# The head of a fused attention and gated-MLP kernel: x tile 0 in halves on two queues, a one-block first weight piece, a new matmul order and a fourth gate/up slot

## Chip, cores, metric

One core of one Trainium2 chip. The metric is the device time of one execution in microseconds, median of several. The kernels ran on several chips; each ran beside the kernel before on its own chip, and is compared with those runs only.

## Reference

```python
xn = layernorm(x)                                  # x: 2048 x 512, bf16
s  = attention(xn @ wq, k_cache, v_cache) @ wo     # 32 heads, 2048 keys, head size 128
h  = relu(xn @ W_gate) * (xn @ W_up)               # 512 -> 1792
g  = silu(h @ W_down)                              # 1792 -> 512
return x + s * g
```

## The kernel before

The kernel runs the MLP first, for four blocks of 512 rows, then the attention. Only the start of the MLP (the "head") is touched. The first block has no normalized x yet, so its four x tiles of 128 rows are only centred (the row scale is applied later), transposed on TensorE into the PSUM banks `ps_acc`, copied by ScalarE (ACT) to `xcT`, and multiplied with the first three column blocks of both weights, tile by tile (`head_tile`). Column block 3 and later ones are full width, 512 columns. The gate and up results stand in three slots of two PSUM banks each.

```python
FCS = [0, min(3, FC), min(8, FC), FC]      # weight pieces: 3, 5 and 6 column blocks
HFC = 3                                    # column blocks that run tile by tile
warm_w = sem_ln1.sig(dve.memset(warm[:], 0.0))
load_x0(sp, 0)                             # x tile 0, 128 KB
load_x0(act, 1)
load_w(sp, Wg_sb, wg_src, sem_wg, 0)       # 384 KB
load_w(act, Wu_sb, wu_src, sem_wu, 0)      # 384 KB
load_x0(sp, 2)
load_x0(act, 3)
load_w(sp, Wg_sb, wg_src, sem_wg, 1)
load_w(sp, Wu_sb, wu_src, sem_wu, 1)
... # x of block 1, the last weight pieces, the other x blocks, W_down: all on sp

def head_ln():
    ctok = {0: head_transpose(0, head_center(0))}
    warm_mm(2)
    for n in range(4):
        if n + 1 < 4:
            ntok = head_center(n + 1)      # DVE: statistics, aggregation, centring
        _wait(pe, ctok[n])                 # xcT copy of tile n
        head_tile(n, 0)
        if n + 1 < 4:
            ctok[n + 1] = head_transpose(n + 1, ntok)
        for fc in range(1, HFC):
            head_tile(n, fc)               # 4 gate and 4 up matmuls, 128 x 128

... # emit_gate_up, for column blocks from HFC on:
s = ring_acquire()                         # waits until slot s has been read out
... # 4 gate matmuls and 4 up matmuls of 128 x 512
... # main:
_wait(pe, warm_w)
warm_mm(10)                                # filler matmuls, 128 x 512, to raise the clock
head_ln()
```

The softmax here doesn't subtract the row's maximum and nothing guards it: scores larger than these inputs give would overflow.

## Time and profile before

| | kernel before |
|---|---|
| median of 3 (range) | 1287.48 us (1286.75 to 1287.56) |
| span of the profiled execution | 1286.0 us |
| TensorE busy | 1279.3 us |
| full-width block 3 starts | 13.63 us |

Two lines of the page: the busy time of each engine, and the chain of work that ended last by engine. PE and PEld are TensorE's matmuls and weight loads, DVE is VectorE, ACT ScalarE, POOL GpSimd, SP SyncE; a q behind a name means the engine's instruction queue.

```profile
PE 1279.3 (99%) x12040; PEld 835.4 (65%) x12040; DVE 382.0 (30%) x685; ACT 1001.7 (78%) x1109; POOL 13.2 (1%) x25
...
PE 98%; DVE 1%; DMA 0%; issue 0%; ACT 0%; ACTq 0%
```

TensorE (PE) bounds the kernel: 98% of the last chain is its work. What it waited for in the whole span fits on five lines (columns: engine, tile and line that waited, what it waited for, then us in total, times, longest):

```profile
PE ps_r L374 <- DVE warm L239: 1.2, 1, 1.2
PE ps_r L402 <- DMA Wu_sb<-in_B_W_up_dram: 0.5, 1, 0.5
PE ps_r L779 <- ACT OT_store L719: 0.4, 1, 0.4
PE ps_r L488 <- ACT gr_sb L454: 0.4, 1, 0.4
PE ps_r L402 <- ACT xcT L369: 0.2, 1, 0.2
```

So there are about 2.7 us of waits in 1287. The timeline of TensorE in the head (start, duration, engine, line, operation, count, and the wait ahead of it; a duration holds some 0.17 us of drain, so the pace is read from the starts):

```profile
1.19 4.23 PE L374 MATMUL ps_r<-warm 128*128 128x512 bf16 x10 [1.19 <-DVE warm L239]
5.26 0.39 PE L364 MATMUL ps_acc<-ident,xc_sb 128*128 128x128 bf16 x4
...
6.33 0.40 PE L402 MATMUL ps_r<-xcT,Wg_sb 128*128 128x128 bf16 x4 [0.25 <-ACT xcT L369]
7.23 0.40 PE L402 MATMUL ps_r<-xcT,Wu_sb 128*128 128x128 bf16 x4 [0.51 <-DMA Wu_sb<-in_B_W_up_dram]
7.46 0.39 PE L364 MATMUL ps_acc<-ident,xc_sb 128*128 128x128 bf16 x4
...
12.82 0.39 PE L402 MATMUL ps_r<-xcT,Wu_sb 128*128 128x128 bf16 x4
13.63 1.02 PE L488 MATMUL ps_r<-xcT,Wg_sb 128*128 128x512 bf16 x4 [0.41 <-ACT gr_sb L454]
```

Warm-ups start 0.427 us apart, the transposes at 5.26 are at the full pace (four in 0.23). The first gate tile starts at 6.33, its up half at 7.23 when the first Wu piece has landed. From there starts follow without a gap, 0.22 to 0.23 for each group of four, to 12.82. Block 3 follows only at 13.63, after a wait for slot 0.

The first DMA issues on the two queues (SP, then ACT; start and duration of the issue alone):

```profile
0.74 0.39 SPq L233 DMA_DIRECT2D x_sb<-in_A_x_dram  x1
1.18 0.42 SPq L227 DMA_DIRECT2D Wg_sb<-in_B_W_gate_dram  x1
```

```profile
0.74 0.41 ACTq L233 DMA_DIRECT2D x_sb<-in_A_x_dram  x1
1.18 0.45 ACTq L227 DMA_DIRECT2D Wu_sb<-in_B_W_up_dram  x1
```

Each issue takes about 0.4 us of its queue, so the second DMA of a queue is issued at 1.18.

### The profile page before, as it was taken

The page shows a single profiled execution, that of the slowest core. Times are in us where ns is not written, and L with a number is a line of the kernel's source. Part 1 is how long each engine was busy: PE and PEld are TensorE (multiplying, and loading weights), DVE is VectorE, ACT ScalarE, POOL GpSimd, SP SyncE. Part 2 cuts the span into 40 slices and gives each one's busy share as a digit, 9 for nine tenths or more (in the row PEclk, how much of TensorE's full clock was granted, in tenths as well). Part 3 has the DMA queues.
Part 4 walks back from the last instruction along what each step waited for, and adds up shares of the span by engine and source line. Part 5 has one row for each costly group of instructions (what it writes and reads, how often), then busy time and mean ns, then how long its engine had stood idle before and what let it go on. Part 6 is the DMA issues. An engine that isn't in the chain of part 4 may idle for free.

```text
span 1286.0 us, 26948 instructions
## 1 busy us (share of the span) xinstructions
PE 1279.3 (99%) x12040; PEld 835.4 (65%) x12040; DVE 382.0 (30%) x685; ACT 1001.7 (78%) x1109; POOL 13.2 (1%) x25
## 2 busy tenths in 40 slices
PE   9999999999999999999999999999999999999998
PEld 5444466666666666666666666666666666666665
DVE  6433311112222222222222222222222222234456
ACT  3322399998888888888888888888888888888884
POOL 2100000000000000000000000000000000000000
PEclk9999999999999999999999999999999999999999
DMA  9600123332222332332221322323323212332302
GB/s 262 131 1 1 21 44 52 63 57 38 37 54 47 71 54 50 55 70 51 54 46 33 64 47 53 55 67 55 55 50 71 54 34 38 52 65 55 50 14 74
DMA packets 240977, 72.13 MB, mean 56 GB/s; under 512 B 227808, under 2 KB 240864, under 8 KB 240864
## 3 DMA queue, kind: packets, MB, share of 16 engines
q1 hardware_dynamic: 240048, 69.76, 28.4%
q8 instruction: 96, 1.57, 0.5%
q10 hardware_dynamic: 816, 0.66, 0.2%
q14 instruction: 17, 0.14, 0.0%
HBM read 32.77 MB, written 2.10 MB: 27 GB/s over the span
## 4 chain that ended last, share of the span: by engine, by line
PE 98%; DVE 1%; DMA 0%; issue 0%; ACT 0%; ACTq 0%
PE ps_acc L742 36%; PE ps_r L645 34%; PE ps_r L578 9%; PE ps_r L599 8%; PE ps_acc L511 4%; PE ps_r L488 4%; PE ps_r L492 4%; PE ps_r L779 1%; DMA Wu_sb<-in_B_W_up_dram 0%; DVE fin_tmp L787 0%; PE ps_r L402 0%; ACT gr_sb L454 0%; DVE x_sb L792 0%; PE ps_acc L364 0%; DVE Onorm L696 0%
## 5 line engine op out<-in xcount | busy, mean ns | idle before, releaser
L655 ACT ACTIVATE PT<-ps_r 128x1024 bf16<-128x1024 f32 x1024 | 952.5, 1054 | 167.7 <-PE ps_r L645 167.7
L742 PEld LDWEIGHTS ps_acc<-V_sb,PT 128*128 128x128 bf16 x8192 | 621.1, 98 | 241.7 <-ACT PT L655 3.5
L742 PE MATMUL ps_acc<-V_sb,PT 128*128 128x129 bf16 x8192 | 776.7, 220 | 0.0
L645 PE MATMUL ps_r<-QT_sb,KT_sb 128*128 128x512 bf16 x2048 | 754.2, 379 | 0.0
L672 DVE RECIPROCAL rz_sb<-ps_acc 128x4 f32<-128x4 f32 x127 | 23.3, 184 | 729.5 <-PE ps_acc L742 729.5
L645 PEld LDWEIGHTS ps_r<-QT_sb,KT_sb 128*128 128x128 bf16 x2048 | 194.9, 98 | 1.1 <-DVE QT_sb L589 0.4
L578 PE MATMUL ps_r<-xnT,Wq_sb 128*128 128x512 bf16 x512 | 130.9, 379 | 0.0
L599 PE MATMUL ps_r<-Wo_sb,OT_store 128*128 128x512 bf16 x448 | 114.6, 379 | 0.0
L589 DVE CAST QT_sb<-ps_r 128x512 bf16<-128x512 f32 x128 | 88.5, 692 | 48.1 <-PE ps_r L578 48.1
L578 PEld LDWEIGHTS ps_r<-xnT,Wq_sb 128*128 128x128 bf16 x512 | 49.9, 97 | 60.6 <-ACT PT L655 27.1
L675 DVE TENSOR_TENSOR Onorm<-ps_acc,rz_sb 128x512 bf16<-128x512 f32 x127 | 87.8, 691 | 4.4
L599 PEld LDWEIGHTS ps_r<-Wo_sb,OT_store 128*128 128x128 bf16 x448 | 43.8, 98 | 52.9 <-ACT PT L655 0.2
L454 ACT ACTIVATE gr_sb<-ps_r 128x512 bf16<-128x512 f32 x56 | 32.9, 595 | 49.9 <-PE ps_r L488 49.3
L612 DVE TENSOR_TENSOR s_acc<-s_acc,ps_r 128x512 f32<-128x512 f32 x96 | 66.0, 688 | 17.3 <-PE ps_r L599 17.3
L460 DVE TENSOR_TENSOR hT<-gr_sb,ps_r 128x512 bf16<-128x512 bf16 x56 | 38.4, 686 | 47.2 <-PE ps_r L492 42.1
L511 PE MATMUL ps_acc<-Wd_sb,hT 128*128 128x512 bf16 x224 | 49.0, 379 | 0.0
L492 PE MATMUL ps_r<-xnT,Wu_sb 128*128 128x512 bf16 x168 | 43.1, 379 | 0.0
L488 PE MATMUL ps_r<-xnT,Wg_sb 128*128 128x512 bf16 x168 | 43.1, 379 | 0.0
L511 PEld LDWEIGHTS ps_acc<-Wd_sb,hT 128*128 128x128 bf16 x224 | 21.9, 98 | 26.4
L519 ACT ACTIVATE sig_sb<-ps_acc 128x512 f32<-128x512 f32 x12 | 7.2, 597 | 29.5 <-PE ps_acc L511 29.5
L488 PEld LDWEIGHTS ps_r<-xnT,Wg_sb 128*128 128x128 bf16 x168 | 16.4, 98 | 19.8
L492 PEld LDWEIGHTS ps_r<-xnT,Wu_sb 128*128 128x128 bf16 x168 | 16.4, 98 | 19.8
(50 smaller groups left out, 182.2 us busy)
## 6 DMA issues: line engine op xcount, KB each, us to landing
V_sb<-in_A_v_cache_dram SPq DMA_DIRECT2D x32, 512.0 KB, 4.8
Wq_sb<-in_A_wq_dram SPq DMA_DIRECT2D x32, 128.0 KB, 2.5
Wo_sb<-in_A_wo_dram SPq DMA_DIRECT2D x8, 512.0 KB, 5.0
OT_store<-Onorm SPq DMA_TRANSPOSE x127, 2.4
Wd_sb<-in_B_W_down_dram SPq DMA_DIRECT2D x1, 1792.0 KB, 14.3
x_sb<-in_A_x_dram SPq DMA_DIRECT2D x3, 512.0 KB, 11.4
out_dram<-x_sb SPq DMA_DIRECT2D x6, 256.0 KB, 2.2
Wg_sb<-in_B_W_gate_dram SPq DMA_DIRECT2D x1, 768.0 KB, 10.9
```

The costliest lines, as they stand in the source:

```text
L460: dve.tensor_tensor(hT[par][:, fc, :], gr_sb[gk][:], ps_r[:, gb + 1, :], ALU.mult)
L488: ins = pe.matmul(ps_r[:, gb, :], Wg_sb[:, c, fs], xT[:, c, xs], start=(c == 0), stop=(c == DC - 1))
L492: ins = pe.matmul(ps_r[:, gb + 1, :], Wu_sb[:, c, fs], xT[:, c, xs], start=(c == 0), stop=(c == DC - 1))
L511: ins = pe.matmul(ps_acc[:, jb, 0:D], hT[par][:, fc, j * 128:(j + 1) * 128], Wd_sb[:, fc, :], start=(fc == 0), stop=(fc == FC - 1))
L578: ins = pe.matmul(ps_r[:, bank, :], Wq_sb[b][:, c, :], xnT[:, c, qs], start=(c == 0), stop=(c == DC - 1))
L589: etok = sem_qpe.sig(dve.tensor_copy(QT_sb[b][:, qs], ps_r[:, bank, :]))
L599: ins = pe.matmul(ps_r[:, bank, 0:D], OT_store[g % 2][:, hh, n * 128:(n + 1) * 128], Wo_sb[g % 2][:, hh, :], start=(hh == 0), stop=(hh == ...
L612: dve.tensor_tensor(s_acc[:, n, :], s_acc[:, n, :], ps_r[:, bank, 0:D], ALU.add)
L645: ins = pe.matmul(ps_r[:, 2 * s + tt, :], KT_sb[h % 2][:, t * 128:(t + 1) * 128], QT_sb[h % 2][:, qs], start=True, stop=True)
L655: act.activation(PT[pb][:], ps_r[:, 2 * s:2 * s + 2, :], ACTF.Exp, scale=scale)
L675: dve.tensor_tensor(Onorm[ob][:], o_ap, rz_sb[:].to_broadcast([128, 4, Dh]), ALU.mult))
L742: ins = pe.matmul(o_ap, PT[pb][:, tt, j * 128:(j + 1) * 128], V_sb[vb][:, t, 0:VW], start=(t == 0 and j % 2 == 0), stop=(t == KT - 1 and j ...
```

## The change

The intent: x tile 0 lands sooner because both queues bring a half of it; the first head tile has to wait only for one column block of each weight (128 KB) instead of three; the matmuls follow the order in which data should arrive; block 3 uses the two accumulator banks, free by then, as a fourth slot; and the warm-ups multiply a constant that exists already, so that they need no memset (nine instead of ten ahead of the transposes, one instead of two after them).

```diff
-                FCS = [0, min(3, FC), min(8, FC), FC]
+                FCS = [0, 1, 3, 8, FC]
-                def load_x0(eng, n):
-                    x0_tok[n] = sem_x0[n].sig(eng.dma_start(x_sb[:, n:n + 1, :], x_t[:, n:n + 1, :]))
+                def load_x0(eng, n, lo=0, hi=128):
+                    x0_tok[n] = sem_x0[n].sig(eng.dma_start(x_sb[lo:hi, n, :], x_t[lo:hi, n, :]))
-                warm_w = sem_ln1.sig(dve.memset(warm[:], 0.0))
-                load_x0(sp, 0)
-                load_x0(act, 1)
+                load_x0(sp, 0, 0, 64)
+                load_x0(act, 0, 64, 128)
+                load_x0(sp, 1)
+                load_w(act, Wu_sb, wu_src, sem_wu, 0)
                 load_w(sp, Wg_sb, wg_src, sem_wg, 0)
-                load_w(act, Wu_sb, wu_src, sem_wu, 0)
-                load_x0(sp, 2)
+                load_x0(act, 2)
+                load_w(sp, Wg_sb, wg_src, sem_wg, 1)
+                load_w(act, Wu_sb, wu_src, sem_wu, 1)
                 load_x0(act, 3)
-                load_w(sp, Wg_sb, wg_src, sem_wg, 1)
-                load_w(sp, Wu_sb, wu_src, sem_wu, 1)
 ... # larger pieces and the x block after them, on sp
                 def head_ln():
+                    c0 = head_transpose(0, head_center(0))
+                    n1 = head_center(1)
+                    warm_mm(1)
+                    _wait(pe, c0)
+                    head_tile(0, 0)
+                    c1 = head_transpose(1, n1)
+                    n2 = head_center(2)
+                    head_tile(0, 1)
+                    _wait(pe, c1)
+                    head_tile(1, 0)
+                    head_tile(1, 1)
+                    head_tile(0, 2)
+                    c2 = head_transpose(2, n2)
+                    n3 = head_center(3)
+                    head_tile(1, 2)
+                    _wait(pe, c2)
+                    head_tile(2, 0)
+                    head_tile(2, 1)
+                    c3 = head_transpose(3, n3)
+                    head_tile(2, 2)
+                    _wait(pe, c3)
+                    for fc in range(HFC):
+                        head_tile(3, fc)
 ... # emit_gate_up
-                        s = ring_acquire()
+                        if Q == 0 and fc == HFC:
+                            s = None                     # the accumulator banks
+                            _wait_all(pe, acc_free)
+                        else:
+                            s = ring_acquire()
 ...
-                _wait(pe, warm_w)
-                warm_mm(10)
+                warm_mm(9)
```

## The prediction

> **What bounds the kernel.** TensorE: on the page it is busy 1279.3 of 1286.0 us (99%), and the chain that ended last is 98% TensorE. The waits view of TensorE over the whole span lists five, 2.7 us together: 1.2 at the start (memset of `warm`), 0.5 (Wu landing), 0.4 (at the first full-width gate matmul), 0.2 (xcT copy), 0.4 (tail). So no edit of the head can win more than some 2 us plus whatever filler work the head holds; 2% would be 26 us. The change touches only the first 14 us.
>
> **The head before (timeline).** Ten warm-up matmuls start at 1.19 and go 0.427 us apart. x tile 0 is landed at 3.30; statistics, aggregation and centring (0.69, 0.18, 0.35) finish at 4.60, but the transposes wait behind the warm-ups until 5.26. The xcT copy ends at 6.26, head matmuls start at 6.33, stand 0.51 for the 384 KB Wu piece (issued 1.18, 6.0 to landing), and from 7.23 TensorE is dense until about 13.0 (12 head tiles of 0.44, four groups of transposes of 0.22). Then 0.41 us of idle for accumulator slot 0: the next full-width group starts at 13.63.
>
> **What the change does, as I cost it.**
> 1. No memset before the warm-ups, nine instead of ten: start near 0.85, so transposes at about 4.7 (was 5.26). Gain 0.5.
> 2. x tile 0 first on both queues: landed at about 2.8 (was 3.25; estimate from 262 KB having moved by about 2.95). Centring would end at about 4.1, so the warm-ups bind and this is mostly hidden.
> 3. First weight piece 128 KB instead of 384: landed well before the first head tile at about 5.85. The 0.51 wait goes.
> 4. New wait: head tile (0, block 1) wants the second piece at about 6.5. 1.18 MB are queued up to it on the two queues; from the rate of before (1.15 MB by 5.7 us, landings about 1 us behind the bytes) it lands near 7.0. The rows are now 256 and 512 bytes instead of 768; the Trainium skill, "DMA: Bandwidth & Descriptors", Specifications, gives 512 B as the least size for line rate, so the 256-byte pieces may move slower (no trace here shows it yet). Loss about 0.5.
> 5. Two head tiles more are ahead of 7.2 than before; the head ends at about 12.2 (was 13.0).
> 6. Fourth slot in the accumulator banks, free since the last xcT copy: block 3 follows without the 0.41 us idle, if blocks 3 to 7 (landed about 11.2 before, perhaps 11.6 now) are there. Gain 0.4 to 0.6.
> TensorE stays dense after that and everything later only shifts.
>
> **Sum.** Block 3 starts near 12.2 instead of 13.63: 1.4 us, all on the critical path. Predicted 1286.1 us, 8 in 10 between 1285.0 and 1287.3. Chances: faster by over 2% 0.005, within 2% 0.99, slower 0.005.
>
> **What would show it.** Timeline after: first warm-up near 0.85, first head tile near 5.85, no wait between the gate and up of tile (0,0), a wait of some tenths at the second weight piece, no idle before block 3, which starts at 11.8 to 12.6; the rest of the kernel shifted by the same amount.
>
> **What would make it wrong.** The clock: the Trainium skill, "TensorE: Matmul & The Clock Gate", Part 1, says TensorE runs at half rate until it was busy for a window of about 3.4 us that runs freely. The trace agrees: warm-ups 0.427 us apart, transposes from 5.26 at 0.057 each. With one warm-up less and a wait at 6.5 the full rate may come later, and head tiles at half rate cost up to 0.44 each. ACT issues five DMAs instead of three; if its table load (1.28 us) then delays the xcT copy, 0.3 is lost. A late second or third piece eats the gain.

## More of the kernel before

The data moved between 3 and 8 us (last three columns: granted TensorE clock, DMA share, GB/s):

```profile
3.00:8.00 5.00, 4.25 (x31) 2.09 (x30) 3.24 (x8) 1.46 (x4) 0.00 (x0) 1.00 1.05 339
```

## The result, and the profile after

The changed kernel took 1291.24 us (median of 5, 1289.08 to 1291.61) beside 1287.52 for the kernel before (5 runs, 1286.75 to 1287.57). The ratio is 1.0027 (95% interval 1.0013 to 1.004). A ratio is the mean time of one kernel's runs over that of the other's of the same rounds, so it is not quite the ratio of the medians. By a threshold of 2% the two are the same, as nearly any change of a 14 us head must be; but the sign is wrong: 3.7 us were lost where 1.4 were to be won, and the time lies outside the predicted range.

The same lines of the page, after:

```profile
PE 1281.3 (99%) x12038; PEld 836.8 (65%) x12038; DVE 381.6 (30%) x684; ACT 1001.5 (78%) x1109; POOL 13.2 (1%) x25
...
PE 98%; DVE 1%; DMA 1%; issue 0%; ACTq 0%; ACT 0%
```

The waits of TensorE after the change:

```profile
PE ps_r L417 <- DMA Wu_sb<-in_B_W_up_dram: 2.4, 1, 2.4
PE ps_r L377 <- PEq L895: 0.8, 1, 0.8
PE ps_r L805 <- ACT OT_store L745: 0.4, 1, 0.4
PE ps_r L417 <- DMA Wg_sb<-in_B_W_gate_dram: 0.3, 1, 0.3
PE ps_r L417 <- ACT xcT L369: 0.2, 1, 0.2
```

The wait for slot 0 is gone, as intended, and so is the wait for the memset (PEq is TensorE's own sequencer: the start of the program). A new wait of 2.4 us for Wu stands in their place. The timeline of TensorE:

```profile
0.78 4.00 PE L377 MATMUL ps_r<-const-bfloat16-1.0 128*128 128x512 bf16 x9 [0.78 <-PEq L895]
...
6.00 0.59 PE L417 MATMUL ps_r<-xcT,Wg_sb 128*128 128x128 bf16 x4 [0.35 <-DMA Wg_sb<-in_B_W_gate_dram]
...
6.87 0.39 PE L417 MATMUL ps_r<-xcT,Wg_sb 128*128 128x128 bf16 x4
9.69 0.47 PE L417 MATMUL ps_r<-xcT,Wu_sb 128*128 128x128 bf16 x4 [2.43 <-DMA Wu_sb<-in_B_W_up_dram]
9.95 0.63 PE L417 MATMUL ps_r<-xcT,Wg_sb 128*128 128x128 bf16 x4
...
13.33 0.39 PE L417 MATMUL ps_r<-xcT,Wu_sb 128*128 128x128 bf16 x4
13.82 0.40 PE L417 MATMUL ps_r<-xcT,Wg_sb 128*128 128x128 bf16 x4
...
15.17 0.39 PE L417 MATMUL ps_r<-xcT,Wu_sb 128*128 128x128 bf16 x4
15.79 0.40 PE L417 MATMUL ps_r<-xcT,Wg_sb 128*128 128x128 bf16 x4 [0.23 <-ACT xcT L369]
...
17.14 1.03 PE L515 MATMUL ps_acc<-xcT,Wg_sb 128*128 128x512 bf16 x4
```

Four things are to be read from it.

1. The head begins earlier: the first gate tile starts at 6.00 (6.33 before).
2. The second Wu piece (blocks 1 and 2) ends a wait at 9.69. The gate tile ahead of it had started at 6.87, so about 2.6 us of issue are lost by start times (9.69 less 6.87 less 0.22).
3. After that wait the groups of four start 0.43 us apart instead of 0.22, until 13.33: eight steps from 9.95 to 13.33 take 3.38 us instead of 1.79, which loses 1.6 us.
4. Two more gaps, 13.33 to 13.82 and 15.17 to 15.79, where a group should take 0.22: 0.27 and 0.40 us for the xcT copy, right after a transpose with a single head tile behind it.

The granted clock in these stretches (window; busy times and counts of the five engines; clock, DMA share, GB/s):

```profile
8.00:9.60 1.60, 0.00 (x0) 0.00 (x0) 0.00 (x0) 0.00 (x0) 0.00 (x0) 1.00 1.06 348
...
10.00:11.00 1.00, 1.00 (x12) 1.00 (x10) 0.53 (x1) 0.00 (x0) 0.00 (x0) 0.50 1.02 350
```

The clock was still full while TensorE stood idle and is at one half right after; by the trace's clock records it was at one half from 9.87 to 13.28, for 3.41 us. Block 3 starts at 17.14 instead of 13.63, 3.5 us later, which is the whole difference of the spans (1289.5 and 1286.0). The sum closes: the losses above make 4.9 us, about 0.2 more is the first gate tile at the lower rate at 6.00; before, the head held 0.7 us ahead of the first up tile and 0.6 ahead of block 3 (starts at 6.33 and 7.23, 12.82 and 13.63, less the 0.22 of the group itself); and the head begins 0.33 earlier. 5.1 less 1.3 less 0.3 is 3.5.

Why is the piece late? The issues on the queues, SP and then ACT:

```profile
0.74 1.19 SPq L232 DMA_DIRECT2D x_sb<-in_A_x_dram  x2
1.99 1.52 SPq L226 DMA_DIRECT2D Wg_sb<-in_B_W_gate_dram  x3
```

```profile
0.75 0.56 ACTq L232 DMA_DIRECT2D x_sb<-in_A_x_dram  x1
1.34 0.87 ACTq L226 DMA_DIRECT2D Wu_sb<-in_B_W_up_dram  x1
...
2.79 0.46 ACTq L226 DMA_DIRECT2D Wu_sb<-in_B_W_up_dram  x1
```

Two issues of x on SP take 1.19 us together, so the first Wg piece is issued at 1.99 instead of 1.18; on ACT the half tile took 0.56 us and the first Wu piece 0.87. The second Wu piece is the fourth issue on ACT, at 2.79, and its landing was waited for until 9.69. Less data moved, too:

```profile
3.00:8.00 5.00, 3.91 (x26) 1.88 (x24) 3.57 (x9) 2.58 (x4) 0.00 (x0) 1.00 0.97 275
```

275 GB/s between 3 and 8 us against 339. So there were three suspects from here on: the ACT queue gets a poor share of the DMA engines (theory A), the short rows of the small pieces move slowly (theory B), and, after the first batch, the order and number of issues on the queues (theory C).

### The profile page after: what moved, and what is told of

It is laid out like the page before. It is cut to its first block, busy times and chain, and to the rows that moved or that the text cites. A ratio compares the mean times of both kernels' runs of the same rounds, so it can differ in the third digit from the quotient of the medians.

```text
span 1289.5 us, 26945 instructions
## 1 busy us (share of the span) xinstructions
PE 1281.3 (99%) x12038; PEld 836.8 (65%) x12038; DVE 381.6 (30%) x684; ACT 1001.5 (78%) x1109; POOL 13.2 (1%) x25
## 4 chain that ended last, share of the span: by engine, by line
PE 98%; DVE 1%; DMA 1%; issue 0%; ACTq 0%; ACT 0%
PE ps_acc L768 36%; PE ps_r L671 34%; PE ps_r L604 9%; PE ps_r L625 7%; PE ps_acc L538 4%; PE ps_r L519 3%; PE ps_r L515 3%; PE ps_r L805 1%; DMA Wu_sb<-in_B_W_up_dram 1%; PE ps_r L417 0%; DVE fin_tmp L813 0%; ACT xcT L369 0%; ACTq L232 0%; ACTq L226 0%; PE ps_acc L519 0%
```

## The experiments

Fifteen kernels ran, all with correct results, all with 5 rounds. "Before" is the median of the 9 runs of the kernel before in the same job. Most single parts move the time by less than the 95% interval of the ratio (about plus or minus 0.13%, 1.6 us), so by the intervals only the full change, e2, e4, e8 and e12 are clear of 1. For the rest I rest on the traces and on how little the 5 and 9 runs of a pair overlap.

| run | what it is | median (range), us | less before, us |
|---|---|---|---|
| after | the full change | 1291.24 (1289.08 to 1291.61) | +3.7 |
| e1 | full change, second Wu piece on SP | 1288.52 (1287.90 to 1288.86) | +1.0 |
| e2 | full change, weight pieces of before | 1290.21 (1289.96 to 1290.72) | +2.7 |
| e4 | full change, fillers ahead of the wait for Wu | 1291.05 (1289.91 to 1293.89) | +3.5 |
| e8 | full change, fillers ahead of the wait for Wg | 1289.72 (1289.65 to 1289.94) | +2.2 |
| e12 | full change, x tiles whole | 1289.03 (1288.21 to 1290.84) | +1.7 |
| e3 | before + fourth slot | 1286.92 (1286.59 to 1287.17) | -0.6 |
| e7 | before + matmul order | 1288.77 (1288.55 to 1289.29) | +1.2 |
| e5 | before + halves | 1288.41 (1288.16 to 1290.77) | +0.9 |
| e11 | before + halves, other access pattern | 1288.47 (1288.12 to 1288.75) | +1.1 |
| e13 | before + halves, Wg second on SP | 1288.84 (1288.68 to 1289.20) | +1.3 |
| e6 | before + weight pieces | 1288.36 (1287.88 to 1289.16) | +0.8 |
| e14 | before + weight pieces, second Wu on SP | 1287.95 (1287.71 to 1288.16) | +0.4 |
| e9 | before + slot + constant warm-ups | 1286.50 (1286.46 to 1287.12) | -0.9 |
| e10 | e9, Wu ahead of x tile 1 on ACT | 1287.15 (1287.07 to 1287.35) | -0.2 |
| e15 | e9, nine warm-ups | 1286.56 (1286.41 to 1286.66) | -1.0 |

### e1: the second Wu piece on the other queue

```diff
-                load_w(act, Wu_sb, wu_src, sem_wu, 1)
                 load_x0(act, 3)
+                load_w(sp, Wu_sb, wu_src, sem_wu, 1)
```

> The changed kernel with one move: the second Wu piece (blocks 1 and 2, 256 KB) is issued on the SP queue behind the second Wg piece instead of on the ACT queue. Theory A (the ACT queue gets a small share of the DMA engines while the SP queue has work, so what is put on it late lands late): the piece lands near 7.5 us instead of 9.64, TensorE waits for it about 0.5 us instead of 2.4, the clock never drops to half, and the time falls by about 3.5 us to the level of the kernel before (1287.5). Theory B (the short rows of 256 and 512 bytes make the whole transfer slow, whichever queue carries it): the piece lands at 9 or later, the clock drops again, and the time stays within 1 us of the changed kernel (1290 to 1291).

Measured: 1288.52, 2.7 us less than the full change. The up tile of block 1 starts at 8.16 instead of 9.69, the clock is 1.000 in all five runs. This speaks for theory A, but the piece landed later than A had said (7.5), and the wait was split: 1.1 us for the two Wg pieces and 0.5 for Wu. The move also took one of five issues off ACT, so it does not tell the share of a queue from the number of its issues.

### e2: the weight pieces of before, the rest of the change kept

```diff
-                FCS = [0, 1, 3, 8, FC]
+                FCS = [0, 3, 8, FC]
 ... # loads: second and third pieces on sp, as before
```

> The changed kernel with the weight pieces of before (3, 5 and 6 column blocks; first Wu piece on ACT, all others on SP), the rest of the change kept: halves of x tile 0, matmul order, fourth slot. If the cutting of the weights is the whole loss, the stall of 2.4 us and the stretch at half clock go, block 3 starts at 12.6 to 13.0 and the time is about 1286.7, under the kernel before. If the new matmul order has a cost of its own (a copy of xcT exposed after the second, third and fourth group of transposes, about 0.35 us each: one head tile of 0.44 does not cover 0.22 of transposes and 0.58 of copy with its two hand-overs), TensorE shows two or three waits for the xcT copy, block 3 starts near 13.7 and the time is about 1287.5.

Measured: 1290.21, a miss for both sides. Without any small piece, and with nothing but x tiles and the first Wu piece on ACT, the kernel is nearly as slow as the full change. TensorE waited 2.4 us, now for the first Wg piece on SP, until 7.87, and the clock was at one half from 8.57 to 11.98:

```profile
7.87 0.38 PE L415 MATMUL ps_r<-xcT,Wg_sb 128*128 128x128 bf16 x4 [2.40 <-DMA Wg_sb<-in_B_W_gate_dram]
...
8.31 0.39 PE L362 MATMUL ps_acc<-ident,xc_sb 128*128 128x128 bf16 x4
8.54 0.59 PE L415 MATMUL ps_r<-xcT,Wg_sb 128*128 128x128 bf16 x4
```

So the clock fell 0.7 us after the wait was over: three groups of four still ran at the full pace. The order's cost was as expected (two waits for the xcT copy). So neither A nor B holds as the whole cause: a large piece on SP can be the late one. What was common to e2 and the full change, and not to the kernel before, was the issue of the first Wg piece at 1.99 instead of 1.18. That is theory C.

### e3: the fourth slot alone

```diff
-                        s = ring_acquire()
+                        if Q == 0 and fc == HFC:
+                            s = None
+                            _wait_all(pe, acc_free)
+                        else:
+                            s = ring_acquire()
```

> The kernel before with the fourth gate/up slot alone. Theory: the wait of 0.41 us ahead of block 3 goes and nothing else changes, so the time falls by 0.4 us (1287.1 if before runs at 1287.5). Rival: the wait comes back one block later, as a wait for slot 0 or 1, and the time stays.

Measured: 1286.92, 0.6 less than before, as the theory said and a little more. The wait ahead of block 3 is gone and comes back nowhere. In this execution the first Wu piece had also landed ahead of its tile, so block 3 started at 12.50: the wait of 0.5 us for Wu in the trace of before is there in some executions only.

### e4: fillers ahead of the wait for Wu

```diff
+                        if n == 0 and fc == 1 and i == 1:
+                            warm_mm(11)
                         if n == 0 and fc in FCS:
                             pe.wait_ge(sems[FCS.index(fc)].h, 16)
```

> The changed kernel with eleven more filler matmuls (128 by 512, 0.216 us each) placed just ahead of the wait for the second Wu piece: the data come no earlier, TensorE is only kept busy. If the stretch at half clock is caused by the idle 2.4 us, it goes, and the 28 head matmuls and 4 transposes that ran 0.107 us apart run 0.056 apart: 1.6 us faster than the changed kernel (about 1289.5), with the wait for the piece ending at 9.6 as before. If the clock drops for another reason, no gain.

Measured: 1291.05, with a range of 4 us. A failed experiment that told something: in this execution it was the second Wg piece, on SP, that came at 9.89, ahead of the fillers, after a wait of 2.7 us. The clock had fallen at 9.21, during that wait. The eleven fillers ran behind it, from 10.29 until the next tile at 13.83 and at the lower pace until 12.63, and cost time. The same loads in the same order make now the one, now the other queue late. That ends theory A in its form "ACT is starved".

### e5: the halves alone

```diff
-                load_x0(sp, 0)
-                load_x0(act, 1)
+                load_x0(sp, 0, 0, 64)
+                load_x0(act, 0, 64, 128)
+                load_x0(sp, 1)
```

> The kernel before with x tile 0 alone changed: in halves on the two queues, tile 1 behind its half on SP. Weight pieces, matmul order and slots are those of before. Theory C (what comes late is what stands behind the extra issue on SP: in the runs so far with halves the first Wg piece is issued at 2.0 to 2.2 us instead of 1.18): the first Wg piece is issued near 2.0, its data land at 7 us or later instead of 6.0, and the time is 0.7 to 2 us above before[...]. Theory A (it is the later pieces on the ACT queue that are starved) and theory B (short rows): neither exists here, so the time is that of before or 0.2 less.

Measured: 1288.41, 0.9 above before, as theory C expected. The issues on SP:

```profile
0.74 1.20 SPq L233 DMA_DIRECT2D x_sb<-in_A_x_dram  x2
1.99 0.42 SPq L227 DMA_DIRECT2D Wg_sb<-in_B_W_gate_dram  x1
```

The first Wg piece is issued at 1.99 and was waited for until 8.62 in the profiled execution (1290.77 us, the slowest of the five, with the clock at one half after a wait of 2.7 us); the other four runs lie between 1288.16 and 1288.43. The issue came 0.8 us later than before, but by the trace's packet records the piece's last packet ended 2.5 us later (7.89 against 5.42; in e11 1.9 later, at 7.33). So the later issue is only a part of the delay. The rest passed between the issue and the last packet, and what took it was not tested. And x tile 0 itself came hardly sooner in the full change: its statistics started at 3.19 us, before at 3.30.

### e6: the weight pieces alone

```diff
-                FCS = [0, min(3, FC), min(8, FC), FC]
+                FCS = [0, 1, 3, 8, FC]
 ... # second Wu piece on act ahead of x tile 3, the rest on sp
```

> The kernel before with the weight pieces alone changed: 1, 2, 5 and 6 column blocks, the second Wu piece on ACT as in the change, x tiles whole as before. Theory A: the second Wu piece lands at 8 or later, so the time is at least 1 us above before. Theory C: the first Wg piece is issued at 1.2 as before, the second pieces land at 6 to 7 us, the wait of 0.5 us of before goes or moves, and the time is within 0.5 us of before.

Measured: 1288.36, 0.8 above before: between the two theories' numbers, and with ranges that overlap (before: 1287.10 to 1288.59). The first tile has no wait for weights any more, but block 1 waits until 8.35 for the second Wg piece (on SP). The wait has moved from 6.5 to 7.6 us and grown.

### e7: the matmul order alone

```diff
 ... # head_ln() of the change, with warm_mm(2) as before
```

> The kernel before with the matmul order alone changed. If one head tile (0.44 us) between transposes and the first tile that needs their copy leaves the copy exposed, there are three waits of TensorE for the xcT copy of 0.39 us each by start times, and the time is 1.1 us above before (1288.6). If the order is free, as the prediction had it, the time is that of before.

Measured: 1288.77, 1.2 above before (1288.6 was expected, 1.1 above); of the five and nine runs only the slowest of before (1288.59) reaches the fastest here (1288.55). The waits for the copy are there three times; the first of them:

```profile
7.39 0.39 PE L364 MATMUL ps_acc<-ident,xc_sb 128*128 128x128 bf16 x4
...
7.83 0.39 PE L414 MATMUL ps_r<-xcT,Wu_sb 128*128 128x128 bf16 x4
8.45 0.40 PE L414 MATMUL ps_r<-xcT,Wg_sb 128*128 128x128 bf16 x4 [0.23 <-ACT xcT L369]
```

The transposes start at 7.39, the one head tile behind them is done by 8.05 (7.83 plus 0.22), and the next tile, which needs the copy of these transposes, starts at 8.45: 0.40 us exposed. Before, two head tiles covered the copy. The order has a cost of its own that has nothing to do with the DMA.

### e8: fillers ahead of both waits

```diff
+                        if n == 0 and fc == 1 and i == 0:
+                            warm_mm(12)
                         if n == 0 and fc in FCS:
                             pe.wait_ge(sems[FCS.index(fc)].h, 16)
```

> The changed kernel with twelve filler matmuls (0.216 us each) ahead of the wait for the second Wg piece, so that they bridge the wait whichever of the two second pieces is late; the earlier attempt had them behind that wait, where they came too late. If the half clock is caused by the idle time, it goes in all runs and the time falls by about 1.7 us (28 to 32 matmuls at 0.056 instead of 0.107 apart) to about 1289.5, the level of the one run of the changed kernel that showed a clock of 1.000 (1289.1). If not, the time stays at 1291.

Measured: 1289.72, all five within 0.3 us and with a mean clock of 1.000. This is what was expected if the clock falls because TensorE stands idle. Its timeline:

```profile
6.82 2.78 PE L377 MATMUL ps_r<-const-bfloat16-1.0 128*128 128x512 bf16 x12
9.44 0.38 PE L419 MATMUL ps_r<-xcT,Wg_sb 128*128 128x128 bf16 x4
```

The twelve fillers run from 6.82, the gate tile of block 1 starts at 9.44 and its up tile 0.22 later, at 9.66, at the full pace. In this execution the data were there sooner than in the trace of the full change (the second Wu piece's last packet ended at 7.19 instead of 9.18), but the fillers held TensorE, so the same up tile starts at the same time (9.66 and 9.69). Block 3 then starts at 15.61 instead of 17.14, 1.53 us sooner. What differs in between is the clock; that it is lost by idling is therefore shown. In the medians (each against before on its chip) 1.5 us is a lower bound, since the fillers hold TensorE even where the data came sooner; the one run of the full change with a clock of 1.000 (1289.08) is 2.2 us under the median of its five, and the trace gave 1.6.

### e9 and e10: the parts that pay, and Wu first

```diff
 # e9: e3, and
-        pe.matmul(ps_r[:, 2 * NSLOT - 1, 0:D], warm[:, 0:128], warm[:], start=True, stop=True)
+        pe.matmul(ps_r[:, 2 * NSLOT - 1, :], ones_w, ones_r, start=True, stop=True)
-                _wait(pe, warm_w)
 # e10: e9, and
-                load_x0(act, 1)
+                load_w(act, Wu_sb, wu_src, sem_wu, 0)
                 load_w(sp, Wg_sb, wg_src, sem_wg, 0)
-                load_w(act, Wu_sb, wu_src, sem_wu, 0)
+                load_x0(act, 1)
```

> The kernel before with the fourth slot and with the warm-up matmuls on the constant ones (no memset, no wait for it; still ten and two). The slot alone gave 0.6 us. The warm-ups then start near 0.78 instead of 1.19, so the transposes, which stood behind them, and all after them start 0.3 to 0.4 earlier, unless the first Wu piece lands later than that: 1286.2 to 1286.9. If warm-ups that start earlier end before the clock has risen, the last ones and the transposes run at half rate and nothing is won over the slot alone.

> The same, with the first Wu piece ahead of x tile 1 on the ACT queue. Theory C (a piece lands late by its place behind other issues): its issue moves from 1.15 to 0.75 us, its landing comes 0.3 to 0.5 earlier, x tile 1 is still there before its statistics at 4.5; the time is that of the run before or up to 0.3 us less (1286.0 to 1286.6), with no wait for Wu in the head. It would be slower if x tile 0 came later by sharing the engines with the piece.

Measured: e9 took 1286.50, 0.9 less than before, inside the expected range. e10 took 1287.15 and missed: no wait for Wu, but TensorE waited 0.4 us for x tile 1, now the later one on ACT. What is moved back on a queue becomes the new wait.

### e11: the halves with another access pattern

```diff
-  eng.dma_start(x_sb[lo:hi, n, :], x_t[lo:hi, n, :])
+  eng.dma_start(x_sb[lo:hi, n:n + 1, :], x_t[lo:hi, n:n + 1, :])
```

> The halves alone, as in the run with halves only, but with the tile axis kept in the access pattern (a slice of length 1 instead of an index), as the kernel before has it. In the run with halves the issues of x took 0.56 to 0.6 us instead of 0.39. If the form of the pattern makes an issue long, the first Wg piece is issued at 1.6 and the time is within 0.5 us of before. If it is the issue of one DMA more and the two queues starting together, it is issued near 2.0 again and the time is 0.9 us above before (1288.4).

Measured: 1288.47, 1.1 above before; the first Wg piece is again issued at 1.99, so the form of the pattern is not it. The half tile took 0.57 us to issue on ACT here too, a whole tile 0.41 before. In this execution TensorE waited 2.25 us for the first Wg piece, until 7.90, and after that the groups went on at the full pace of 0.22 us: the clock did not fall. After the 2.4 us in the full change and in e2, it did; the length of the wait is not the whole of it, as the table under "Why the prediction was wrong" shows.

### e12: the full change with whole x tiles

```diff
-                load_x0(sp, 0, 0, 64)
-                load_x0(act, 0, 64, 128)
-                load_x0(sp, 1)
+                load_x0(sp, 0)
+                load_x0(act, 1)
+                load_w(sp, Wg_sb, wg_src, sem_wg, 0)
                 load_w(act, Wu_sb, wu_src, sem_wu, 0)
-                load_w(sp, Wg_sb, wg_src, sem_wg, 0)
-                load_x0(act, 2)
+                load_x0(sp, 2)
 ... # load_x0 with a slice for the tile axis, as in e11
```

> The changed kernel with the x tiles loaded as before (whole, tile 0 and 2 on SP, 1 and 3 on ACT); the small weight pieces on both queues, the order and the slot stay. Theory C: the first Wg piece is issued at 1.2, the second pieces land at 7 to 8.3, the wait for them is at most 1.5 us, the clock does not drop, and the time is about 1288.7 (2.5 us under the changed kernel; from the single parts: 1287.5 plus 0.8 for the pieces, plus 1.2 for the order, less 0.6 for the slot). If the halves have no share in the loss of the full change, it stays at 1290.5 to 1291.5.

Measured: 1289.03, 2.2 less than the full change, near the 1288.7 of the sum. Three runs lie at 1288.2 to 1289.0 with a mean clock of 1.000; two, 1290.0 and 1290.8, have 0.999, which fits one stretch at half clock (half of 3.4 us in 1290 is 0.0013), though single runs of the kernel before show 0.999 as well. In the profiled one (1288.21) the wait for the second pieces was 0.6 us. So the halves carry most of the loss, partly because without them the wait mostly stays short enough for the clock; but in two of five it probably fell still, which the expectation had not allowed for.

### e13: halves, with the first Wg piece second on SP

```diff
-                load_x0(sp, 1)
                 load_w(sp, Wg_sb, wg_src, sem_wg, 0)
+                load_x0(sp, 1)
```

> The kernel before with x tile 0 in halves on the two queues, but the first Wg piece second on SP and x tile 1 third. Place on the queue: the piece is issued near 1.35 us and lands near 6.2, TensorE waits for it or for Wu at most 0.7 us, and the time is within 0.3 us of before (1287.2 to 1287.8). The half tiles themselves: the piece lands at 7 or later all the same and the time stays near 1288.4. x tile 1 then lands later, near 5, which may cost up to 0.4 us through its statistics, as in the run with Wu first.

Measured: 1288.84, 1.3 above before. The piece is issued at 1.38 and no longer waited for; to that extent its later issue was the cause. But x tile 1, now third, came in time for statistics at 7.11 only, and TensorE waited for its centring:

```profile
PE ps_acc L365 <- DVE xc_sb L355: 0.9, 1, 0.9
```

With halves there are three DMAs that the head needs at once on SP (the half, tile 1, the piece), and the third of them is late. The time expected under "place on the queue" (within 0.3 us) was a miss, because the price of a late tile 1 was put at 0.4 us at most and was 0.9.

### e14: the pieces, with the second Wu piece on SP

```diff
 # e6, and
-                load_w(act, Wu_sb, wu_src, sem_wu, 1)
                 load_x0(act, 3)
+                load_w(sp, Wu_sb, wu_src, sem_wu, 1)
```

> The kernel before with the weight pieces of 1, 2, 5 and 6 blocks, the second Wu piece on SP behind the second Wg piece. Queue: if the ACT queue is what makes the second pieces late, the waits shrink and the time falls from 1288.4 to at most 1287.8. Short rows: the data moved between 3 and 8 us stay near 300 GB/s[...], the second Wu piece lands at 7.5 or later, and the time stays at 1288.0 to 1288.8.

Measured: 1287.95, 0.4 above before, half of what e6 lost; between the two expectations again. The rate from 3 to 8 us is 304 GB/s, that of e6 300. So the queue and the rows may each have a share in it, but with e6 and e14 on two chips and their ranges overlapping neither is shown. Nor does the lower rate belong to short rows alone: with rows of 768 bytes the kernels with whole x tiles moved 339 to 358 GB/s, those with halves 304 to 320 (e2, e5, e11, e13). Even in the better place the small pieces win nothing.

### e15: one warm-up less

```diff
-                warm_mm(10)
+                warm_mm(9)
```

> The fourth slot and the constant ones with nine warm-ups ahead of the first transposes instead of ten. If TensorE is held up by the warm-ups, the transposes come 0.3 to 0.4 us earlier (about 4.6, when xc of tile 0 is ready) and the time falls by up to 0.35 us to about 1286.2, unless the first Wu piece, which landed between 5.5 and 7.2 in the runs so far, then binds: no gain in that case. If the clock rises later with fewer warm-ups, it is slower by some tenths.

Measured: 1286.56, 1.0 less than before, ratio 0.9992 (0.998 to 1.0005); its five runs (1286.41 to 1286.66) lie under all nine of before (1287.09 to 1287.79). e9 on its chip was 0.9 less, so the warm-up that was taken away is worth nothing here:

```profile
5.19 0.96 PE L375 MATMUL ps_r<-const-bfloat16-1.0 128*128 128x512 bf16 x2
6.21 0.38 PE L403 MATMUL ps_r<-xcT,Wg_sb 128*128 128x128 bf16 x4
```

In this execution the two fillers after the transposes ran at the lower pace (two in 0.96 us, in e9 0.84, in the kernel before 0.59), and the first head tile starts at 6.21 (e9: 6.30). What the missing warm-up gave, the slower fillers took in part. e9 and e15 are the best versions found, equal within their scatter. By their medians both beat the kernel before and the changed one; by the intervals neither is clear of the kernel before, and only e15's runs lie under all of those.

## Why the prediction was wrong

**What held.** The kernel is bound by TensorE, the head is all that changes, and everything after block 3 only shifts: 3.5 us at block 3, 3.5 us in the span. The fourth slot takes away the wait ahead of block 3 (e3, 0.6 us). The memset-free warm-ups start at 0.78, and slot and constant together give 0.9.

**The step that failed is point 4**, "it lands near 7.0 ... Loss about 0.5". The wait for the second piece lost 2.6 us in the trace, five times the estimate: the Wu tile that needs it started at 9.69. The estimate counted bytes in front of the piece at the rate of before. In one execution it was nearly right: in the trace of e8, with the same loads, the piece's last packet ended at 7.19. What the runs showed in its place:

- The place on a queue. Halving x tile 0 puts a second DMA ahead of the first Wg piece on SP, and each issue takes 0.4 to 0.6 us there; the piece was issued 0.8 us later, in e2, e5 and e11 too, and in the slowest of these executions (e5) the first head tile, which needs it, started at 8.62 instead of 6.33. With the piece moved forward, tile 1 is late (e13). The halves alone cost 0.9 to 1.1 us. As they put 64 KB more ahead of the piece as well as an issue, the two are not told apart.
- Less data moved between 3 and 8 us: 275 GB/s instead of 339. The small pieces alone bring it to 300 (e6), the halves alone to 304 (e5) or 320 (e11), so it is not the short rows alone. The pieces alone cost 0.8 us (e6), or 0.4 with the second Wu piece on SP (e14).
- What the halves were to buy (point 2) is nearly nothing: tile 0's statistics started 0.1 us sooner, not 0.5. Point 3 held only in part: the gate tile at 6.00 still waited 0.35 us for its 128 KB (0.5 to 0.7 in the traces of e1, e4 and e8).

**The clock was named as a risk and not put into the sum.** The text had it under "What would make it wrong", at up to 0.44 for each head tile. But the risk named was that the full clock comes late. What happened is that it was granted and lost again for 3.4 us, which cost 1.6 us in the trace and at least 1.5 by e8. The clock records of the traces (the list of its changes, in the packed trace) show when. Its first steps, in us:

| trace | full clock from | TensorE idle in the next 3.41 us | then |
|---|---|---|---|
| e4 | 5.80 | 2.6 | half clock, 9.21 to 12.63 |
| after | 6.46 | 2.4 | half clock, 9.87 to 13.28 |
| e2 | 5.15 | 2.4 | half clock, 8.57 to 11.98 |
| e5 | 4.69 | 2.2 | half clock, 8.11 to 11.52 |
| e11 | 4.20 | 2.0 | stays full |
| e13 | 5.24 | 1.5 | stays full |

The steps lie 3.41 us apart, and the clock fell where 2.2 us or more of one such stretch were idle. The wait of e11 is nearly as long as that of e2 (2.25 against 2.40), but 0.3 us of it fell into the next stretch. So the length of a wait does not decide alone; where the stretches lie differs from trace to trace (the first full clock came between 3.49 and 7.17). This is worked out from one trace of each kernel; in the traces not listed less was idle, and the clock stayed full. It fits that two different single repairs (e1, e12) each win over 2 us: the longest waits for data in their traces are 0.7 and 0.6 us, and the clock stayed full. The other risk named, ACT's table load, cost nothing: the xcT copy ended at 5.84, before the gate tile could start.

**The order was costed at nothing.** The prediction followed the data through the new order, but not the xcT copy: a single head tile (0.44 us) stands between a group of transposes and the tile that needs their copy. Three exposures of 0.4 us, 1.2 us in all (e7). In the trace of the full change only two are seen, 0.7 us together; the first is hidden in the wait for the second piece.

**The sum closes.** Slot -0.6, order +1.2, halves +0.9, pieces +0.8, constant warm-ups -0.3 (e9 less e3, on two chips) make +2.0; e8, the full change without the loss of clock, measured +2.2. The full change is +3.7; the rest, 1.5, is the clock. That the parts add up so well is in part luck: in the full change some of their waits cover each other (the first exposed copy lies within the wait for Wu), and taking the halves out of it wins 2.2 (e12) where they cost 0.9 alone.

**What stays open.** Why the same loads land up to 2 us apart from one execution to the next: the second Wu piece, with the same issues, let the up tile start at 9.69 in the full change, while in the trace of e8 its last packet ended at 7.19. In the slow executions the shares of the 16 DMA engines spread: in the trace of the full change the first engine completed its share of the piece at 6.46, the last at 9.24. Which engine is late and why was not settled. Nor why a half tile takes longer to issue (0.57) than a whole one (0.41). So that the halves and the pieces made the data late is shown; how is not.

## What to carry to other kernels

At a kernel's start, count the issues that stand in front of a transfer as well as the bytes: a tile split over two queues adds an issue, and the transfer behind it pays. A wait of TensorE of 2.4 us cost another 1.6 us in clock here, so a change that may lengthen a wait to some 2 us should be costed with that, or bridged with filler work. And when matmuls are reordered, follow each operand's whole way (transpose, copy, hand-over) through the new order, not only its arrival from memory.

## What the Trainium skill lacked or had wrong

- "TensorE: Matmul & The Clock Gate", Part 1, gives the return to the half clock as coming after at least one idle window of about 3.4 us. Here TensorE was never idle for that long: the clock fell where 2.2 us (e5), 2.4 (full change, e2) or 2.6 (e4) of a stretch of 3.41 us were idle, and not where 2.0 were (e11). That the low clock then lasts for one window is confirmed: it is at one half from 9.87 to 13.28, and the pace of 0.43 us lasts from 9.95 to 13.33.
- "DMA: Bandwidth & Descriptors", section "Issuing engines are not separate DMA queues", says that issuing from several engines saves only the sequencer's time to initiate a DMA, "which is usually small relative to the DMA itself". Against one whole DMA it is small here too: 0.4 us of the 2.5 us from the issue of x tile 0 to its landing. But the issues of one queue follow each other, and at 0.4 to 0.6 us each they take as long as 128 KB need at the 339 GB/s of the kernel before (0.39 us). With one more in front the first Wg piece was issued 0.8 us later and the kernel lost 0.9 us (e5), though not by the issue alone. The passage does not count this sum.
- The same page, Specifications, gives 512 bytes as the least size for line rate. Nothing here speaks against it. By the packet records, rows of 256 bytes took 18 ns each in every trace that has them (14 bytes per ns), rows of 512 bytes moved at 16 to 19 bytes per ns and rows of 768 at 15 to 21, as means over one piece. So the shortest rows are the slowest, and between 512 and 768 bytes no difference is shown.
- No page has that the DMA of a half tile (64 rows) takes longer to issue than that of a whole one (0.57 against 0.41 us on ACT, e11 and before; 0.58 against 0.39 on SP, e13 and before), nor how far the shares of one DMA may spread over its 16 engines (2.8 us in the full change).
